# A parallel attention and MLP block: score maxima and v turned on VectorE, key blocks regrouped for it, and a two-class transfer list

## The chip, the cores and the metric

The kernel runs on one core of a Trainium2 chip. Its time is the device time of one execution in microseconds (us), given as the median over several executions. TensorE (PE) does the matrix products, VectorE (DVE) and ScalarE (ACT) the element-wise work, GpSimd (POOL) some additions, and SyncE (SP) only issues transfers. ACT issues transfers too, from the same queue as its other instructions.

## The reference

```python
x = A_x                                   # 1 x 2048 x 448, float32
xn = _layernorm(x, axis=-1)
return x + _A_ref(xn, A_wq, A_wk, A_wv, A_wo) + _B_ref(xn, B_w1, B_w2)

# _A_ref: 16 heads of 28, one k and one v for all of them
q = (x @ wq) as 16 heads;  k = x @ wk;  v = x @ wv
scores = einsum("bhqd,bkd->bhqk", q, k) * 28 ** -0.5
p = softmax(scores);  o = einsum("bhqk,bkd->bhqd", p, v)
return o.reshape(B, S, 448) @ wo

# _B_ref: dense layer with 1792 hidden columns
return relu(x @ w1) @ w2
```

Everything is float32 outside; inside, the products use values split in a high and a low part.

## The kernel before

The 2048 rows are cut in four query blocks of 512 (`NQB`), the 16 heads in four groups of four (`NHG`). A unit `u` is one query block with one head group; there are 16 units, and each works through 16 key blocks of 128 (`NKB`). TensorE's array is used as four groups of 32 rows, one head (or one slice of a product) in each, and the four groups run at the same time.

There are three stages. In the first (0 to 62 us) the rows are normalised and transposed, and q, k and v are projected; the results go out to DRAM (`qscr`) and come back in the layout that the heads need. k stands in `kHL`, high and low part, one column per key; `kD` holds differences of two blocks of 512 keys. In the MLP stage (62 to about 387 us) the 168 tiles of the two dense layers are worked off, and between their matmuls stand 426 of the 1024 matmuls that serve the scores' row maxima, and eight early score tiles. The attention stage (about 388 to 996 us) makes the scores, their exponentials and the products with v, with the other 598 maxima matmuls between; then the end follows.

The row maximum of the scores is needed before the exponential. `max_mm` (L563) multiplies one unit's high-part queries (`qhi`) by 512 keys into a PSUM bank, and a VectorE reduction (L567) takes the maximum over the keys. With the pair form, ACT writes `more` = relu of a product with `kD` (L758) and VectorE combines it with the first bank (L571). When a unit's 64 pieces are done, `max_final` (L574) makes the negated maxima and their rounding remainder, 128 partitions by 32 values, and orders the next `qhi`. `max_rows` (L583) turns these on PE (L588) into 32 rows by 128, ACT copies them out of the bank (L590), and four transfers (L596) put them into two spare rows of each head's part of the query tile `q`; there the third matmul of a score tile, 30 rows high, adds them to the scores. `v_rows` (L537) turns v from rows by head dimension to key order: four PE transposes (L541) and an ACT copy (L543) into `vtile`.

The order of the work is written out by hand. The table `ROWS` (L32) is read one character at a time in the MLP stage: `a` to `h` start tiles on the four row groups, `0` to `3` go on with one matmul, `i` to `l` and `m` to `t` are maxima matmuls, `vA`, `vB`, ... take a job from the list of owed VectorE work, `A` to `D` start early scores, and one `X65` does the maxima rows of unit 0 and v. The table `ORDER` (L116) gives the attention stage: `B4.12.0.3541602` is a burst of 4 score tiles, with maxima matmuls ahead and behind on the named row groups, and the banks; `V` is the product with v for one key block (L827), `R` one `max_rows`, and `r`, `n`, `O`, `f` normalise and project the output.

Transfers (L448) go out on SP's queue, but in the MLP stage they are put on the list `later`, and every tile that ends (`go_on`, L766) issues the first of that list from ACT's queue. The weights' parts `stg`, the unit queries `qhi`, the query tiles `q` and the eight pieces of v share that list. When a tile of the first layer ends, ACT writes the hidden values' high part (`hH` L716) and VectorE the low part (`hL` L718); of the second layer ACT copies the tile (`y` L725) and POOL adds it (L726). Then its bank is free.

Of the kernel before, what the change touches and what calls it, by code (L numbers as in the profile page):

```python
# [17 lines left out]
NU = NQB * NHG  # L18
P_BUFS = 24
# [11 lines left out]

ROWS = """  # L32
    a3b4c5012012012012012d60123012301230123013o73e5s130g4f330213021p2021t0vA021021021p1021t7021vAl0021e6
    10j2vBh40k7f530g313vA021302130vA21302130213vA02130213m021l2q121e4g6vA02h302302vAj730230j12302vA3j202
    3023vA0230k03vAf6h51313vBm713q113vA13i21313vAi013131vBc4a320b120vBd212031203120vA31c03123e4f3vA2l701
    201h1201vA3201320132e2vAj53023j60h42vA03g3j703203f02vAe131203210l521vA0l6g210210h32vA1a7321320132vA0
    13g103120l52f402l61021h0vA02130c313201vA32f20321i5321i1321g7vA31a61230f3230vA120l5120l41021vAl1e0210
    2f60l22vA10h32130k513vA01c4301230f723vA012l1012h6012vA3c2e31320312vA031203120h41vA2031k5i131g63e223j
    0vA0230b32h70213vA02130k513e4vA130c11302103vA201320132i6132m01h22q53f4vA23123e31231vA03k61010h1vAb5c
    703120312vA0312031203120f23k0103k41e53k6vA1031g30h71203vA02f13023123vA1i0321i4h521a23vA210321032013v  # L40
    Ak60130k01h3e71k4vA30f20g531023vA102310231e12vA31203f7k60310k0130g2vA1d4201320132vA0b5320132301c6vA0
    l012h212e4312vB0312031203vA1023102l7m312q0d12vAf431g5a23120312031032vA10h62n7032r0e1320j3320f232013v
    B2013g40132i01vA23e5123f1021l30vA21h20c7130213vA021302f63201320l01g10l4120l312vAe712021h502vA130g210
    321032vA1i032j4a123f7023vA10c33102310vA23102d01e623j2023f102310vB23102130213vA01k430j230f33vA0g11h72
    01321e0vA321032310231k50vAp410t210h1vAc601301320b7321302vA13201h32m513q21g03f623m4123q1123e71230vA12
    031023j2023vAb102h61i5312vAe331k4301g73102vA3f002l2102h110vA2310231k503vA1c430123012h7vA0123e6123023
    10g13b20231vA02h40123a5123vA012301o33013s70d01c6301230123012302vAf43201l7g21012e1l31vA20h61023f5023v
    A10230123e412301l7201l3201l10g0vA102h21e623102vA3102023j70k4vA3b30g531e0231vA02310231021vA30f620p112
    t7vAe212h310231023103k4f003vA1c70312h501230vA123102j6320g3j1302b43vAe7213021302vA1302130c0102vAp6e31
    2t10120h712vA03120312032i23b1vA32a51h402103vA1k6031013k30f73vAe0k21301g13120vA312031203f52vA0p61201t  # L50
    30g41d202130123023n7e12vA3r30230f02h5012301320132e2vA31k60310h110k3vA301k7301g53e412vA3012302f2l60vA
    21l3201h010c1vA3101302b7302vA13201230123m5g213q6213e121302vA1d3021302103vAo6103s43vA3g7f1m5312q2312a
    031vA2031201d42032vA0f330231m2231q6231i5h1g013213e72vB132013201320vAl61g402l5102h0vA0b22301230123vA0
    1g3313021p1e42j5t602f00h721032vA103210321e2vA32103j62030f4k5301c1vA0132e3123102d0vA1203b62031g2032vA
    103210321032102310k5310o731e1s4h2vA10310g03032j5vA032032e62l3vB02f1021l4vA021d501230123vA10o2303s7f0
    03vAc31h102310231e52310vA23012301g6l4012l7012h3a2vA12301302f5302vA130213021l1e021l4021h20vAf33013k70
    13g5vA0132013210h6vA2j10320f23210k43vA1e3c73102310vB231023b102310vA23i51g2d412e7321vB0231023102310vA
    k0310k3313vA1o5a2f73s6013vAg101d0201301230123vAe4j3230j6320f2h72vA1032130213vA02130g01302b5l3021h120
    132vA10321i63g21i732f4i32vA31e023102310vA2310g53012l60vA12i7h2213e121vA32013k30130f0vA3k601h5g4013vA
    120312031320vAb73201d220132i3132e513021vB30b620310g731vA0231231i02vA31212i31d1c5vAe2132031203vA21032  # L60
    n4302r0h70g6j3302f130213vB02130213021h5vAi0132j33e7230f22vA3012301g1l401vA20l021e5h6210vA32102310k33
    01vAc730123e11203vAn4203r02032f503g210d312e73120312vA031203b02031vA20p112e6t41201h72013g301320132vA0
    31203120p521vA0t4k1f7010g0d2vB1e321023102vA31023n4023r10vA2323m5f323q7123a61c1vA301201h0201320vAf223
    0123m713q41g63i5123e121032vB1032103210p3vA01k5t4e01h603f1vAk7031g2031230vB123012p410vA2t50f62l7012h1
    01320vB132a3132013vAc503b720120vA120d42e2132013g3012301230123012301230o6130s0f5310h3g710312e43123012
    vA30n1230r02h50vA2j63023f302310vB23103c210l021vA021h7e52j63023vAf402310k1301c3vA30213e221032vA103210
    2310k0l610c5l11e72h3vA1203f22031203vA12301g43012l0vA012h50j6230f3vA32013210321vAa13210h22103j0203f5v
    Ac60310231e332vA1021h1021302vA30j7230b023e513vA021l20210l4g110vA2l3012e6d712301vA23012301c23vA01230f
    12l5012l4120h0vA12031g703120vA3f22i3123a5123012vA301k4301k130f630vAk31e7h21031vA0g0310231023vA0132i4
    1h52i1312e231vA2031203f7203vA120h610k331i4g513e0213vA20j13203j220vA32b3031c7031vA2031201d4201vA320f5  # L70
    320132vA1e33120310231023vAj10o203s63e7c0vA0h30j5320f432vA301232013201vAd1k601301k2301g3vA320132e0132
    vA0l5120h71203f1vAk60130g413i212vA31231m523f0vAq323123e112031201l6021p2vA0f72t301h01vA3e4k5130g11302
    1vB30213201d320vA132031k6031c530b023vA0120d221321e3vA2310301k1301vAo6031s7031e53vA1c4031203f320l1120
    vA120h012e231k7vA031k603f4031k1vA301301g3vA13021302f5302vA12l7012h401g03i61vA23i1132f232m3vA132h512q
    731vA23e41230123013201vAp60c710t121e02120d32b5032103g2103123012vA3012h70j4230j1320f332vA01321e53210d
    6vA2103c4103f702vA310231e3231023102103vA2j1032032e7j0h5vA023j20g33f6023vB10231023e412d1vA012301g5302
    31vA230123012l7012d001g130j2vA230b3231023vA1e623120l71k50h41g003j2vA203f1203120vA3120312103g3vA1203j
    7203f02i5312e1l2vA1201g60120vAl7120f4h32031vA2i5312e03120vA31203120l212vA0d110c73e3132vA0132031203b5
    2vA01201l22e1120vA12010l0210vAd6c30132e7132vA03120321302f1l4o201h5s01031g60vA12301230f323012vA30123m
    41g13q012312e63f72020l2120h31g503vA10231i03213vA2i4132i112vA1d22e3132013vA02f6302130k013vA0k41h7e513  # L80
    01g2vA30j12302b330vA2132013201vA3k0103k6103c4f20vA120d112e3312vA0312031023vA0n0230r623e22vA30j7203g3
    0320vBf420d5123e121vA302130o6130s7130o2h310s03103g510321320vA1320b7d0021vA32e41301k6310g131023vAf502
    l3102l2102h71vA023103123f002vA310231e52l610k31h40k2130vAg7f103210321e0vA32013201230vA1k6301c330123e7
    vA210l5210d220132vB0b63g001321e32vA31023021302vA130k5130k413i71c1vA21h3a02130vA23f2023102310vAg63012
    l51e12l4102h0vA013201320132vA0132m7312q5f3h12i413g213213e6vB12301320f0l52vA01l4201210vA210l3210d72f1
    3vA01k53013g001vA32e2132012h6j40vA230f72310k33vA10c531021302vA1320b132013201g73i412d0e521302vC130213
    02130vA1o3301s4e73103vAk2f503103g110vB210d6123e0123vA032j4032j2032j70vAh5203203f62vA301c33102310vA2h
    110213a42j2302j730g0j530vA203f320132e6vA132013201302vA1h402n2302r73vAe12j5303g6032f00vBh3210321032vA
    3102310g43210l7210l52102d21vAe32301c630132vA0f432013201d7vA21i5321e23210vA32j1032032vA03b30c013i4213
    vA2e6132012l501vA2l10f2g7012h31vA02310231032vA103f02031201l42i5121e32h6vA10g23j10203f72vA03120321e03  # L90
    vA2103k4013g3013201vA23012a5l1120l2120h0vA1c4032f603201vA32e7132013201h5o1013s3013c2031230123012h401
    vA230j0320f532a3132vB103210210l1vA10f40h21k0vA031g503120132vA1032b60321vA2i731c1e4312031vA203120h3n0
    203r5203f2g6i72312e131vB203120312031vAk50310o431e6s7vA10l001h1g301320vBb532013i7213vAe2213012h61023v
    Aj0032f13021302vA130g51l4201d720132vA0f3320132a013k6031c4l1012vBh50123012301vA2301230132vA01l620f721
    02vBp21e51t10g010h4vA1203j602302b33e72vA1032103210vA3210321032n1a53k60r2h30g7f0302vA310230123e421vA3
    201h50k21301g33012vA30213021320p6120t1j7c20f52h0012vB31e3213021032vA103k1f403c70132e2vA1230123012302
    1d60g510321i1321e732vA102301230f2c33vA01230123i0123vA1i12h7123j5vAe623b430213021vA3021h20k01310vA3k1
    f703103g41vA0321h3021302vA13i52b0321i2g631vAi1123e41230123vA0n7230r5230vA2h00b2321e33210312vA301o130
# [71 lines left out]
def attention_plus_mlp(ctx: ExitStack, tc: tile.TileContext, x, wq, wk, wv, wo, w1, w2, out):  # L170
# [412 lines left out]
    def max_rows(b, between=None):  # L583
# [7 lines left out]
        if between:  # L591
            between()
# [389 lines left out]
```

## Time and profile before

| | |
|---|---|
| median of three runs | 1009.01 us (1007.97 to 1009.62) |
| profiled execution | 1007.41 us |
| its span, first to last instruction | 1005.6 us |
| mean granted TensorE clock | 0.998 |
| PE busy | 995.6 us, 99% |
| DVE busy | 714.6 us, 71% |
| ACT busy | 699.9 us, 70% |
| POOL busy | 248.5 us, 25% |
| DMA, share of 16 engines | 10.3% and 3.1% on the two largest queues |

Busy times are read from one profiled execution. Matmuls overlap and their ends are modelled, so a high share of PE busy time does not say that PE works at its peak. In a row such as `L611 PE MATMUL b<-q,kHL 28*128 28x512 f32` the line of the program comes first, then the engine, the operation, what is written and from what, and the tile. `b` and `o` are PSUM banks. ACTq is the queue of transfers that ACT issues; a row of it says how long the queue was held by the issue.

### The profile page before, as it was taken

What the parts mean: (1) busy time and instruction counts of PE and PEld (TensorE: products, weight loads), DVE (VectorE), ACT (ScalarE), POOL (GpSimd) and SP (SyncE); (2) the same over time, 40 slices, a digit from 0 to 9 for tenths busy, and PEclk for the clock granted to TensorE, in tenths of its full rate; (3) what the DMA queues carried; (4) which work ended last, traced back from release to release, by engine and by line L of the source; (5) the groups of instructions that cost most, each with busy time, mean ns of one, the idle gap of its engine ahead of it and who ended that gap; (6) DMA issues with size and microseconds to landing.
All of it is one profiled execution on the core that took longest, in us unless ns stands there. A gap on an engine that the chain in (4) does not pass through costs nothing.

```text
span 1005.6 us, 28502 instructions
## 1 busy us (share of the span) xinstructions
PE 995.6 (99%) x11704; PEld 634.0 (63%) x11704; DVE 714.6 (71%) x1287; ACT 699.9 (70%) x1359; POOL 248.5 (25%) x251
## 2 busy tenths in 40 slices
PE   9999999999999999999999999999999999999998
PEld 8779999999998996444444445444445443445444
DVE  7649888888887877888888876778775545774202
ACT  5533344434333447888899987899998799997994
POOL 4325464655646335110110110110110110110110
PEclk9999999999999999999999999999999999999999
DMA  7742101101010011101011002010011110000001
GB/s 242 255 138 83 41 13 41 25 30 41 15 41 13 3 34 34 34 24 41 5 44 34 23 33 63 10 44 23 23 34 37 36 34 23 13 13 29 22 13 37
DMA packets 28391, 43.76 MB, mean 44 GB/s; under 512 B 9140, under 2 KB 20084, under 8 KB 28260
## 3 DMA queue, kind: packets, MB, share of 16 engines
q1 hardware_dynamic: 22336, 32.68, 10.3%
q10 hardware_dynamic: 5924, 9.26, 3.1%
q8 instruction: 91, 1.49, 0.6%
q14 instruction: 40, 0.33, 0.1%
HBM read 29.36 MB, written 12.18 MB: 41 GB/s over the span
## 4 chain that ended last, share of the span: by engine, by line
PE 98%; DVE 1%; DMA 1%; ACT 0%; issue 0%; ACTq 0%; POOL 0%; POOLq 0%
PE o L827 25%; PE b L611 25%; PE b L701 23%; PE b L563 9%; PE b L867 4%; PE o L701 4%; PE b L424 3%; PE b L231 1%; PE b L433 1%; PE b L373 1%; PE o L563 1%; PE b L402 0%; DMA qscr<-qs 0%; PE b L588 0%; PE b L911 0%; DMA qhi<-qscr 0%
## 5 line engine op out<-in xcount | busy, mean ns | idle before, releaser
L567 DVE TENSOR_REDUCE nmx<-b 128x1 f32<-128x512 f32 x860 | 551.6, 685 | 154.6 <-PE b L563 130.9
L614 ACT ACTIVATE p<-b 128x512 f32<-128x512 f32 x1016 | 522.6, 611 | 73.1 <-PE b L611 69.5
L611 PE MATMUL b<-q,kHL 28*128 28x512 f32 (+1 forms) x3072 | 335.6, 425 | 0.0
L563 PE MATMUL b<-kHL,qhi 28*128 28x512 f32 x917 | 327.6, 449 | 1.4 <-ACT more L758 1.1
L611 PEld LDWEIGHTS b<-q,kHL 28*128 28x128 f32 (+1 forms) x3072 | 196.5, 183 | 186.6 <-DVE nmx L567 101.2
L701 PE MATMUL b<-xt,w 32*128 32x512 f32 x2058 | 300.2, 393 | 0.0
L701 PE MATMUL b<-w,hH 32*128 32x448 f32 x1552 | 277.9, 369 | 0.0
L827 PE MATMUL o<-p,vtile 128*32 128x512 f32 x2032 | 267.1, 605 | 0.0
L701 PEld LDWEIGHTS b<-xt,w 32*128 32x128 f32 x2058 | 242.9, 183 | 4.1 <-SPq L705 1.0
L701 PE MATMUL b<-w,hL 32*128 32x448 f32 x776 | 211.6, 363 | 0.0
L701 PEld LDWEIGHTS b<-w,hH 32*128 32x128 f32 x1552 | 202.4, 183 | 5.8 <-DVE hL L718 0.9
L563 PEld LDWEIGHTS b<-kHL,qhi 28*128 28x128 f32 x917 | 148.5, 183 | 58.3 <-DVE nmx L567 23.0
L726 POOL TENSOR_TENSOR acc<-y,acc 128x448 f32<-128x448 f32 x112 | 128.0, 1153 | 154.0 <-ACT y L725 153.8
L851 POOL TENSOR_TENSOR on<-rb,oS 128x512 f32<-128x512 f32 x15 | 19.2, 1283 | 518.7 <-DMA rb<-rscr 316.3
L701 PEld LDWEIGHTS b<-w,hL 32*128 32x128 f32 x776 | 122.6, 183 | 0.3
L725 ACT ACTIVATE y<-b 128x448 f32<-128x448 f32 x97 | 52.6, 546 | 92.9 <-PE b L701 76.7
L827 PEld LDWEIGHTS o<-p,vtile 128*32 128x32 f32 x2032 | 42.2, 108 | 77.5 <-issue 71.3
L701 PE MATMUL o<-xt,w 32*128 32x512 f32 x294 | 74.2, 394 | 0.0
L701 PE MATMUL o<-w,hH 32*128 32x448 f32 x240 | 69.9, 370 | 0.0
L758 ACT ACTIVATE more<-b 128x512 f32<-128x512 f32 x55 | 32.8, 599 | 39.1 <-PE b L563 23.2
L701 PEld LDWEIGHTS o<-xt,w 32*128 32x128 f32 x294 | 51.8, 183 | 0.3
L571 DVE CUSTOM_DVE_ANT_0 more<-b,more 128x512 f32<-128x512 f32 x57 | 38.9, 686 | 17.2 <-ACT more L758 16.8
(119 smaller groups left out, 764.0 us busy)
## 6 DMA issues: line engine op xcount, KB each, us to landing
qscr<-qs SPq DMA_DIRECT2D x16, 512.0 KB
q<-qscr SPq DMA_DIRECT2D x12, 512.0 KB
rb<-rscr SPq DMA_DIRECT2D x60, 64.0 KB
out<-acc SPq DMA_DIRECT2D x16, 224.0 KB
acc<-in_A_x SPq DMA_DIRECT2D x14, 224.0 KB
qhi<-qscr SPq DMA_DIRECT2D x11, 256.0 KB
stg<-in_B_w ACTq DMA_DIRECT2D x5, 448.0 KB
q<-qscr ACTq DMA_DIRECT2D x4, 512.0 KB
```

The source lines that it names most:

```text
L424: nc.tensor.matmul(pq, w, xm, start=n == 0, stop=n == len(steps) - 1)
L563: nc.tensor.matmul(pm, qhi[u][rows, s * P : (s + 1) * P], k, start=True, stop=True)
L567: nc.vector.tensor_reduce(dst, pm, axis=AX.X, op=ALU.max)
L571: nc.vector.tensor_tensor_reduce(more, pm, more, 1.0, LEAST, ALU.add, ALU.max, dst)
L611: nc.tensor.matmul(ps, kHL[rows, kt, w, keys], qst[u][rows, s, :], start=k == 0, stop=k == 2)
L614: nc.scalar.activation(p, ps, AF.Exp, scale=SCALE)
L701: mm = nc.tensor.matmul(o, w, m, start=self.left == self.n_mm - 1, stop=self.left == 0)
L725: nc.scalar.activation(y, self.ps[:, 0:D], AF.Copy)
L726: nc.gpsimd.tensor_tensor(a, y, a, op=ALU.add)
L758: nc.scalar.activation(more, d[1], AF.Relu)
L827: nc.tensor.matmul(o_acc[u][RB * j : RB * (j + 1)], vtile[:, kb, :], ps[j], start=kb == 0, stop=kb == NKB - 1)
L867: nc.tensor.matmul(py[:, 0:D], om[:, i * P : (i + 1) * P], wm, start=n == 0, stop=n == len(steps) - 1)
```

## The change

Maxima: `max_final` turns its 128x32 result on VectorE in squares of 32 (L583 of the new program) into `rows`, and four transfers write it to a DRAM tile `nscr`; `max_rows` is now two transfers from `nscr` into `q`. It takes no bank, no PE and no ACT operation. For the first three units it is put on the list at once, after two empty entries (`pause`); the others' stand as `R` in `ORDER`, 13 of them.

v: one VectorE transpose of 128x512 in squares of 32 writes `vtile`, and the fourth query tile is loaded right after it into the freed buffer. For that the key blocks are regrouped: a block of 128 is 32 keys from each of the four blocks of 512, so `kHL` and `kD` have other shapes, and `k_diff` makes the differences in eight POOL operations instead of two.

Transfers: `soon` stands beside `later` and is emptied first; `qhi` and the weights' parts go there. The first three query tiles come ahead of the eight pieces of v on `later`.

Buffers: the exponentials go to three tiles of eight slots instead of 24 single buffers and one for the early ones. Both tables are new throughout: 421 maxima matmuls in the MLP stage and 603 after it; the kinds and counts of all other matmuls are the same but for the 20 transposes.

```diff
-    nc.gpsimd.memset(vtile, 1.0)
-    kHL = cst.tile([P, NQB, 2, QB], F32R, name="kHL")
-    kD = cst.tile([P, NQB // 2, QB], F32R, name="kD")
+    kHL = cst.tile([P, 2, NKB, NQB, RB], F32R, name="kHL")
+    kD = cst.tile([P, 2, TPB, NQB, RB], F32R, name="kD")
...
+    def k_diff(b):
+        hi = kHL[:, 0, :, b].bitcast(F32).rearrange("p (t h k) q -> p t h k q", t=2, h=2)
+        for t in range(2):
+            nc.gpsimd.tensor_tensor(kD[:, t, :, b], hi[:, t, 1], hi[:, t, 0], op=ALU.subtract)
...
-            later.append(lambda: nc.scalar.dma_start(dst, src))
+            (soon if first else later).append(lambda: nc.scalar.dma_start(dst, src))
...
-            transfer(qhi[u].bitcast(F32), queries(u)[:, 0])
+            transfer(qhi[u].bitcast(F32), queries(u)[:, 0], True)
...
-    nc.gpsimd.memset(vt, 0.0)
+    nc.gpsimd.memset(vt, 0.5)
+    for u in range(3):
+        load_q(u)
     for b in range(NQB):
         for g, n in kparts:
...
             transfer(vt[d0 : d0 + n].rearrange("p s q -> p (s q)"), src)
-    load_q(0)
-    load_q(1)
-    load_q(2)
+    pause = [lambda: None] * 2
     later.append(lambda: nc.gpsimd.tensor_tensor(vt[:, 0], vt[:, 0], vt[:, 1], op=ALU.add))
+    later += pause
-    def v_rows(b):
...
+    def v_rows():
+        nc.vector.transpose(vtile.rearrange("p k d -> p (k d)"), vt[:, 0])
+        load_q(3)
+
+    later.append(v_rows)
...
-        nm2[u] = t
+        rows = small.tile([P, RB], F32, name="rows")
+        nc.vector.transpose(rows, t.rearrange("p j s i -> p (j s i)").bitcast(F32))
+        dst = nscr[u].rearrange("j s (i x q) -> x (j s i) q", x=HG, q=RB)
+        for x in range(HG):
+            transfer(dst[x], rows[RB * x : RB * (x + 1)])
+        if while_mlp and u < 3:
+            later.extend(pause)
+            max_rows(u)
         load_qhi(u + 3)
...
+    def max_rows(u):
+        for s in range(2):
+            dst = qst[u].bitcast(F32)[:, 0].rearrange("(j c) q -> j c q", c=RB)
+            transfer(dst[:, DH + s], nscr[u, :, s])
...
+    def score_exp(ps, i):
+        nonlocal n_p
+        if n_p % 8 == 0 and len(p_buf) < 3:
+            p_buf.append((ppool if len(p_buf) == 1 else wpool).tile([P, 8, QB], F32, name="w"))
+        p = p_buf[n_p // 8 % 3][:, n_p % 8]
+        n_p += 1
...
-                        transfer(dst, src)
+                        transfer(dst, src, True)
...
-            if later:
-                later.pop(0)()
+            if soon or later:
+                (soon or later).pop(0)()
```

The order at the first use of unit 6's queries, on PE before. `w`, `xt`, `hH` and `hL` belong to MLP tiles, `b0` to `b7` and `o` are banks, and the number behind a name tells one buffer from another:

```order
L701 MATMUL b6_6429<-w_5539,hL_6360 128x448
L701 MATMUL b3_6472<-w_5539,hH_6359 128x448
L701 MATMUL b0_6370<-xt_353,w_5539 128x512
L701 MATMUL b1_6349<-xt_353,w_5539 128x512
L701 MATMUL b4_6494<-w_5539,hH_6359 128x448 [waits SP_sequencer_49]
L701 MATMUL b3_6472<-w_5539,hL_6360 128x448
L701 MATMUL b4_6494<-w_5539,hH_6359 128x448
L701 MATMUL b0_6370<-xt_353,w_5539 128x512
L701 MATMUL b1_6349<-xt_353,w_5539 128x512
L563 MATMUL o_6607<-kHL_76,qhi_6560 128x512 [waits DMAHW0_49,Activation_49]
```

The first of these rows ends the tile in bank b6. On ACT before, the tile's copy and the transfer that its end issues:

```order
L725 ACTIVATE y_6479<-b5_6333 128x448 [waits PE_49,Pool_49]
L758 ACTIVATE more_6552<-o_6550 128x512 [waits PE_49]
L725 ACTIVATE y_6592<-b6_6429 128x448 [waits PE_49,Pool_49]
L450 DMA qhi_6560<-qscr_65 128x512
L716 ACTIVATE hH_6617<-b1_6349 128x512 [waits PE_49]
```

On ACT now, the transfer of unit 6's queries is `qhi_6347`:

```order
L720 ACTIVATE hH_6362<-b3_6089 128x512 [waits PE_49]
L454 DMA qhi_6347<-qscr_65 128x512
L720 ACTIVATE hH_6362<-b1_6105 128x512 [waits PE_49]
L454 DMA nscr_67<-rows_6345 32x32 [waits DVE_49]
L729 ACTIVATE y_6417<-o_6253 128x448 [waits PE_49,Pool_49]
L454 DMA nscr_67<-rows_6345 32x32 [waits DMAHW5_49]
```

It follows the tile in bank b3 (`b3_6089`), whose last matmul is PE's row 4083; the first use of `qhi_6347` is PE's row 4246. Before, the two stand nine rows apart.

The order in the attention stage, on PE before, behind a burst, with the transpose of one unit's maxima:

```order
L563 MATMUL b5_8908<-kHL_76,qhi_6560 128x512
L563 MATMUL b1_8911<-kHL_76,qhi_6560 128x512
L588 MATMUL b6_8914<-ident_72,nm2_5319 32x128
L827 MATMUL o_8554<-p_8802,vtile_73 32x512
L827 MATMUL o_8554<-p_8783,vtile_73 32x512
```

On DVE now, where a unit's maxima are finished:

```order
L569 TENSOR_REDUCE nmx<-b_8719 128x1
L579 TENSOR_REDUCE nm<-nmx 128x16
L580 CAST nm_8723<-nm 128x4x4
L581 TENSOR_TENSOR nm_8723<-nm,nm_8723 128x4x4
L583 STREAM_TRANSPOSE rows<-nm_8723 128x32
L569 TENSOR_REDUCE nmx<-b_8749 128x1
```

The PE row between the burst and the products with v is gone, and VectorE has one row more per unit.

The order on ACT where v and unit 0's maxima are turned, before:

```order
L758 ACTIVATE more<-b_7849 128x512
L590 ACTIVATE rows<-b_7882 32x128
L543 ACTIVATE vtile<-b_7886 128x4x4x28
L596 DMA q<-rows 2x4x128 x4
L725 ACTIVATE y<-b_7805 128x448
L450 DMA q<-qscr 128x1024
```

On ACT now, at the query load that follows v's transpose, much earlier in the MLP stage:

```order
L729 ACTIVATE y<-b_1461 128x448
L720 ACTIVATE hH<-b_1406 128x512
L454 DMA q<-qscr 128x1024
L720 ACTIVATE hH<-b_1419 128x512
L454 DMA stg<-in_B_w 128x3x256
```

The copies out of the banks and the four transfers in a row are gone; the query load waits there for VectorE's transpose of v.

More of the change, by code (lines that the diff above doesn't have):

```diff
@@ L198, in attention_plus_mlp @@
     rscr = dram.tile([NU, HG, QB], F32, name="rscr")
+    nscr = dram.tile([NU, HG, 2, QB], F32, name="nscr")
     acc = cst.tile([P, NT, D], F32, name="acc")
@@ L442, in queries, with transfer @@
         return qscr[g, b]
-    later = []
+    later, soon = [], []
     while_mlp = False
-    def transfer(dst, src):
+    def transfer(dst, src, first=False):
         if while_mlp:
-            later.append(lambda: nc.scalar.dma_start(dst, src))
+            (soon if first else later).append(lambda: nc.scalar.dma_start(dst, src))
         else:
@@ L575, in max_final @@
         nm = small.tile([P, HG, 1, TPB], F32, name="nm")
-        t = small.tile([P, HG, 2, TPB], F32R, name="nm2", bufs=NU)
+        t = small.tile([P, HG, 2, TPB], F32R, name="nm2")
         nc.vector.tensor_reduce(nm, nmx.pop(u), axis=AX.X, op=ALU.max, negate=True)
@@ L799, in attention_plus_mlp @@
             owe_combine(first_of.pop(r), max_mm(b, r, kD))
-        elif c == "v":
+        else:
             owed.pop(ord(b) - ord("A"))()
-        else:
-            v_bank = next(stream)
-            max_rows(b, lambda: v_rows(v_bank))
-            load_q(3)
-            p_early = wpool.tile([P, 8, QB], F32, name="w")
-    for issue in later:
+    for issue in soon + later:
         issue()
```

309 lines of the change are left out of this document (141 added, 168 removed).

## The prediction

> **What bounds the kernel now.** First the busy times and the chain of waits on the page.
>
> ```profile
> span 1005.6 us, 28502 instructions
> PE 995.6 (99%) x11704; PEld 634.0 (63%) x11704; DVE 714.6 (71%) x1287; ACT 699.9 (70%) x1359; POOL 248.5 (25%) x251
> PE 98%; DVE 1%; DMA 1%; ACT 0%; issue 0%; ACTq 0%; POOL 0%; POOLq 0%
> PE o L827 25%; PE b L611 25%; PE b L701 23%; PE b L563 9%; PE b L867 4%; PE o L701 4%; PE b L424 3%; PE b L231 1%; PE b L433 1%; PE b L373 1%; PE o L563 1%; PE b L402 0%; DMA qscr<-qs 0%; PE b L588 0%; PE b L911 0%; DMA qhi<-qscr 0%
> ```
>
> TensorE (PE) is the path from end to end, so two things can shorten the span: PE work that goes, and the few holes in PE. The windows of the MLP stage show where the holes are (columns: window, its length, then busy us and instructions of PE, PEld, DVE, ACT, POOL, then clock, DMA share, GB/s).
>
> ```profile
> 212.00:262.00 50.00, 50.00 (x879) 48.15 (x875) 44.41 (x82) 17.77 (x32) 27.14 (x25) 1.00 0.10 28
> 262.00:312.00 50.00, 47.56 (x839) 45.99 (x835) 41.32 (x78) 19.89 (x36) 27.43 (x25) 1.00 0.09 27
> 305.00:308.30 3.30, 0.86 (x20) 0.46 (x12) 0.45 (x3) 0.54 (x1) 1.82 (x2) 1.00 0.25 79
> ```
>
> A full window holds 879 matmuls in 50.00 us, 57 ns each. The next holds 40 fewer, and its hole lies at 305: 3.30 us with 0.86 of PE, 2.44 us lost. The chain of waits there, and at a smaller hole later (columns: start, us, what):
>
> ```profile
> 305.45 0.02 ACT y L725
> 305.48 2.63 DMA qhi<-qscr
> 308.11 0.14 issue
> 308.25 0.47 PE o L563
> ...
> 352.18 0.02 issue
> 352.21 1.29 DVE nmx L567 x2
> 353.50 0.65 DVE hL L718
> 354.15 0.01 issue
> 354.16 0.46 PE o L563
> ```
>
> At 305.48 ACT issues unit 6's queries (qhi), and PE needs them nine rows of its order later. At 354.16 the wait is VectorE's (DVE's), for a bank that hL frees.
>
> **Removed: the late queries, −2.5 us.** In the changed order the same transfer is issued 163 PE rows ahead of its first use, 163 × 57 ns = 9.3 us, against 2.63 + 0.14 us of transfer: the hole goes, 2.44 us. The other units' transfers stand as far ahead or further. What cures it is the new table: the owed list was empty when this transfer was issued (ACT issued it as soon as its tile ended), so overtaking by itself would have moved nothing there. The hole at 354 is about 0.4 us (between 0.2, PE's idle time there, and 0.7, the matmuls missing at 57 ns); its order goes too, but DVE at 44.41 of 50 us stays as full, so it may come back elsewhere. I take −0.3.
>
> **Removed: transposes on PE.** Sixteen of the units' maxima (L588), four of v (L541). ACT's timeline around one in the attention stage, at another one, and at the place in the MLP (start, us, engine, line; in brackets idle before):
>
> ```profile
> 494.68 2.07 ACT L614 ACTIVATE p<-b 128x512 f32<-128x512 f32 x4 [0.27 <-PE b L611]
> 496.96 2.06 ACT L614 ACTIVATE p<-b 128x512 f32<-128x512 f32 x4 [0.21 <-PE b L611]
> 498.88 0.26 ACT L590 ACTIVATE rows<-b 32x128 f32<-32x128 f32 x1
> 499.55 2.06 ACT L614 ACTIVATE p<-b 128x512 f32<-128x512 f32 x4 [0.40 <-PE b L611]
> 501.84 2.07 ACT L614 ACTIVATE p<-b 128x512 f32<-128x512 f32 x4 [0.23 <-PE b L611]
> ...
> 361.41 0.27 ACT L590 ACTIVATE rows<-b 32x128 f32<-32x128 f32 x1 [1.05 <-PE b L588]
> 361.84 0.54 ACT L543 ACTIVATE vtile<-b 128x448 f32<-128x448 f32 x1 [0.17 <-PE b L541]
> 361.85 2.84 ACTq L596 DMA_DIRECT2D q<-rows  x4
> 365.43 0.55 ACT L725 ACTIVATE y<-b 128x448 f32<-128x448 f32 x1 [3.04 <-PE b L701]
> 365.45 0.33 ACTq L450 DMA_DIRECT2D q<-qscr  x1
> ```
>
> ```profile
> L588 PE MATMUL b<-ident,nm x16: 283/284/285, 361.1 to 945.1; 128*32 128x128 f32 x16
> 571.22 2.07 ACT L614 ACTIVATE p<-b 128x512 f32<-128x512 f32 x4 [0.18 <-PE b L611]
> 573.79 2.06 ACT L614 ACTIVATE p<-b 128x512 f32<-128x512 f32 x4 [0.39 <-PE b L611]
> 576.04 2.07 ACT L614 ACTIVATE p<-b 128x512 f32<-128x512 f32 x4 [0.18 <-PE b L611]
> 894.71 16.93 ACT L614 ACTIVATE p<-b 128x512 f32<-128x512 f32 x32 [0.16 <-PE b L611]
> 911.50 0.26 ACT L590 ACTIVATE rows<-b 32x128 f32<-32x128 f32 x1
> ```
>
> Groups of four exponentials start 2.28 us apart (494.68 to 496.96) and 2.29 (499.55 to 501.84), but 2.59 with a transpose between: 0.30 us, about L588's own 0.284 us; at the other place 2.57 (571.22 to 573.79) against 2.25. Fifteen of these stand in the attention stage. Some (911.50) fall where exponentials run back to back, 16.93 us for 32, so that ACT paces and only part of the 0.28 counts: I take 0.24 each, −3.6, between 0.1 (−1.5) and 0.30 (−4.5). In the MLP one of L588 and the four of v stand together. They cost between 0.28 us, L588 alone with v's hidden, and 1.2 us, ACT's idle times before L590 and L543 (1.05 + 0.17); I take −0.6. The ACT queue is then shut 2.84 us for four small transfers, and that ends too.
>
> **Added on VectorE: +0.6.** Sixteen 128x32 transposes and one of 128x512, which no trace here shows. Nearest rows:
>
> ```profile
> L567 DVE TENSOR_REDUCE nmx<-b 128x1 f32<-128x512 f32 x860 | 551.6, 685 | 154.6 <-PE b L563 130.9
> L579 DVE TENSOR_TENSOR nm<-nm,nm 128x16 fp32r<-128x16 f32 x16 | 4.5, 283 | 0.6
> L559 DVE MEMSET nmx<- 128x64 f32 x16 | 1.8, 112 | 0.0
> ```
>
> A small operation takes 0.11 to 0.28 us, one over 512 elements 0.69. DVE is 71% busy and its results are late for PE only in places, so of 16 × 0.11–0.28 = 1.8–4.5 us I count 0.3 us (from 0, all of it in DVE's idle time, to 4.5). The large one is followed at once by the issue of the fourth query transfer on ACT, which waits until DVE has turned v, since both use one buffer: what is queued behind it on ACT is the next Relu, for which PE waits with a bank. 0.69 us and whatever DVE has in hand, with ACT idle more than half the time: +0.3 (0 to 1.5). By the Trainium skill ("VectorE: DVE Perf Modes", The three transpose paths) DVE turns a 128x128 bf16 tile in 311 ns and TensorE in 390, in squares of 32 only; by that estimate a 128x32 piece would be under 0.31 us and the sum unchanged; no run shows it yet.
>
> **Moved to ACT's queue: +0.6.** In the MLP stage the maxima of five units now leave by 20 transfers to DRAM, and three units' come back by six: 26 where there were 4, one for each tile that ends. The four cost 2.84 / 4 = 0.71 us each on the queue; 22 × 0.71 = 16 us. Almost all of it lies in ACT's idle time (17.77 to 19.89 of 50 us busy), but a Relu queued behind one comes up to 0.7 us late, and PE and DVE's hL wait for it. Bounds: 0, as tiles end 1.9 us apart and banks leave slack, and 16 us. The row nearest to it is the place at 361.85: ACT shut for 2.84 us cost PE less than 1 us, 0.25 a transfer at most with all four in a row; apart they have slack each time. I take 0.03 each.
>
> **Moved between stages: +0.5.** The tables hold 421 early maxima matmuls for 426, 603 late ones for 598. Early they cost 57 ns each, −0.3. Late, L563's mean is
>
> ```profile
> L563 PE MATMUL b<-kHL,qhi 28*128 28x512 f32 x917 | 327.6, 449 | 1.4 <-ACT more L758 1.1
> ```
>
> 0.449 us, four at a time, 0.11 at the least; with its place in a burst of four row groups not always filled I take 0.16: +0.8.
>
> **At nothing.** The queries now leave ahead of v. Two stretches of the chain early in the MLP stage, and the ACT queue's row that the second names:
>
> ```profile
> 63.33 3.74 DMA qscr<-qs
> ...
> 75.94 0.66 ACTq L450
> ...
> 77.27 0.70 DVE hL L718
> ```
>
> ```profile
> 75.35 1.25 ACTq L450 DMA_DIRECT2D q<-qscr  x1
> ```
>
> A v piece shuts the queue 1.25 us, a query tile 0.33 (365.45): up to 1.25 − 0.33 = −0.9, since the Relu and hL behind it were late for PE. But the first pair of maxima now stands ten matmuls nearer to the 3.74 us wait at 63.33, which stays: 10 × 57 ns = +0.6. I take 0. The key differences, eight smaller POOL operations for two, lie in POOL's idle time (22.86 of 50 us), with the first maxima that read them as cover. SP's small transfers (70 for 60) have the time of two units as theirs. Without that lead one would cost what qhi did, 2.6 us a unit.
>
> **Sum.** −2.5 −0.3 −3.6 −0.6 +0.6 +0.6 +0.5 = −5.3 us. The profiled execution took 1007.41 us (span 1005.6, 1.8 outside it) and would take 1002.1. It is 1.6 us below the median of 1009.01; against that median the sum gives 1003.7, which I predict.
>
> **The rivals.**
> *The new table has holes of its own.* A different order of 9,600 matmuls, with DVE at 41–44 of 50 us; for it, the old table has holes at 305 and at 354. Against it, the two full windows quoted have no hole in PE beside the one at 305, and each transfer of the new order stands well ahead of its use. Three new holes of 1.7 us would bring it to 1008.8: no change. 0.17.
> *Slower: ACT's queue in the MLP stage.* Every small transfer delays a bank. At 0.71 us each in full it is 16 − 0.6 us more than in the sum, 1019; the gain is used up at 0.03 + 5.3 / 22 = 0.27 us a transfer, about what the four in a row cost. Against it: ACT is idle over 60% there. Chance of 0.27 or more 0.12, then about 1013. The Trainium skill ("DMA: Bandwidth & Descriptors", Rules for kernel authors) would have many small transfers coalesced and calls those under 64 KB mostly overhead; 32x32 pieces are 4 KB, so by it this is the side to watch; the 2.84 us for four agrees.
> *The DVE transposes take the place of PE's.* If each of the 11 late ones delays the next maxima by its 0.28 us, 3.1 us come back: 1006.5, at the border. 0.09.
> *It does not do what it says.* If the query transfer is late for another reason (its buffer, not its place), the hole at 305 stays: 1006.2. The trace has ACT's y end and the issue together, so 0.05.
>
> **How the numbers follow.** The forecast has 0.57: from 999.5 (transposes 4.5, queue, DVE and tables at their lower ends) to 1006.5. Differences within 0.2%, 2.0 us, can't be told from none here, so faster means below 1007.0. Faster: 0.57, 0.10 of the 0.14 that the two cases near 1006 have, and 0.04 of the first rival: 0.71. Same: 0.13 of that rival, 0.04 of those two and 0.01 of the slower one: 0.18. Slower: 0.11. For 8 in 10 the range runs from 999.3 to 1009.5.
>
> **What would show it.** No PE wait for qhi; PE at 50 of 50 us in the window around 305; exponentials 2.3 us apart where a unit's maxima return, as elsewhere; STREAM_TRANSPOSE under 0.3 us; ACT's queue with gaps after each small transfer, PE's chain without an ACT row behind one. Wrong would be PE idle on Relu or y behind an nscr transfer, a hole where v is turned, or bursts that wait for DVE behind a transpose.

## The result and the profile after

The changed kernel took 1001.52 us (median of four, 1000.93 to 1001.63), the kernel before 1008.86 us (four, 1007.97 to 1009.62): a ratio of 0.9926, interval 0.9909 to 0.9944. Run again beside three of the experiments, it took 0.994 of the time before (0.9925 to 0.9955). The forecast was 1003.7 us, faster. The profiled execution took 1001.45 us against 1007.41, 6.0 less where the sum had 5.3.

The page of the changed kernel, its first lines and the chain by engine (lines answer to those shown of before; L825 is now the product with v, L607 the scores, L705 the MLP, L565 the maxima):

```profile
span 999.2 us, 28738 instructions
PE 990.1 (99%) x11684; PEld 631.4 (63%) x11684; DVE 720.4 (72%) x1304; ACT 696.3 (70%) x1339; POOL 249.9 (25%) x256
PE 97%; DVE 2%; DMA 1%; ACT 0%; issue 0%; ACTq 0%
```

PE is still the path; VectorE has 2% of the chain where it had 1%. The same window as before around 305 us, then the groups of the new operations (minimum, median, maximum in ns; ACT queue rows first, then the two sizes of VectorE transpose):

```profile
262.00:312.00 50.00, 50.00 (x883) 48.07 (x879) 42.57 (x82) 20.61 (x37) 29.60 (x27) 1.00 0.09 28
```

```profile
L454 ACTq DMA_DIRECT2D nscr<-rows x20: 308/314/467, 146.3 to 353.9; - x20
L454 ACTq DMA_DIRECT2D q<-nscr x6: 483/514/564, 163.0 to 261.2; - x6
...
L583 DVE STREAM_TRANSPOSE rows<-nm x16: 211/211/213, 142.3 to 937.9; 128x32 f32<-128x32 f32 x16
...
L544 DVE STREAM_TRANSPOSE vtile<-q x1: 702/702/702, 100.7 to 100.7; 128x512 f32<-128x512 f32 x1
```

The hole is gone: 883 matmuls where there were 839. A small transfer holds ACT's queue 0.31 us outward and 0.51 back, not the 0.71 taken from four in a row. The transposes have the sizes that were bounded, 0.21 and 0.70 us.

Where the span's 6.4 us went, by the starts of the MLP's last matmul with `hL` and of the last product with v:

| | before | changed | difference |
|---|---|---|---|
| start to the last `hL` matmul | 386.9 | 383.2 | −3.7 |
| from there to the last product with v | 608.5 | 605.8 | −2.7 |

The second line holds something that isn't work. In windows of the kernel before (the last three columns are clock, DMA share, GB/s), and of the changed one:

```profile
390.00:400.00 10.00, 10.00 (x77) 4.97 (x73) 8.27 (x16) 7.25 (x15) 3.35 (x4) 0.83 0.39 84
392.00:395.00 3.00, 3.00 (x25) 1.76 (x23) 2.98 (x5) 2.98 (x7) 1.35 (x1) 1.00 0.19 31
395.00:399.00 4.00, 4.00 (x30) 1.41 (x29) 2.29 (x5) 2.25 (x5) 0.00 (x0) 0.59 0.83 184
399.00:402.00 3.00, 3.00 (x35) 1.20 (x31) 2.32 (x5) 2.25 (x5) 1.98 (x2) 0.98 0.01 2
```

```profile
390.00:400.00 10.00, 10.00 (x107) 4.01 (x99) 9.44 (x19) 7.26 (x15) 3.53 (x2) 1.00 0.38 83
```

Before, the granted clock falls to 0.50 for 3.4 us at 395 us, which is 0.83 over the ten: a loss of 1.7 us. In the changed kernel's profile it does not, neither there nor in the MLP stage. So of the 2.7 us only 1.0 is work, and of the whole 6.4 about 4.7. The executions say the same by their mean clock. Where the changed kernel was run again, those of before with a clock of 0.998 took 1008.0 to 1008.5 us (seven), those of the changed kernel with 0.998 took 1003.2 to 1003.9 (four), and its one with 1.000 took 1001.4. At equal clock the change is worth about 4.8 us. The experiments below are compared "at 0.998" or "at 1.000" in the same way.

### The profile page after: what moved, and what is told of

The parts are those of the page before. It is cut to its first block, busy times and chain, and to the rows that moved or that the text cites. A ratio compares the mean times of both kernels' runs of the same rounds, so it can differ in the third digit from the quotient of the medians.

```text
span 999.2 us, 28738 instructions
## 1 busy us (share of the span) xinstructions
PE 990.1 (99%) x11684; PEld 631.4 (63%) x11684; DVE 720.4 (72%) x1304; ACT 696.3 (70%) x1339; POOL 249.9 (25%) x256
## 4 chain that ended last, share of the span: by engine, by line
PE 97%; DVE 2%; DMA 1%; ACT 0%; issue 0%; ACTq 0%
PE o L825 25%; PE b L607 25%; PE b L705 24%; PE b L565 10%; PE b L865 4%; PE b L428 3%; PE o L705 3%; PE b L437 1%; PE b L370 1%; DVE nmx L569 1%; PE o L565 1%; PE b L399 0%; DMA qscr<-qs 0%; DMA acc<-in_A_x 0%; PE b L909 0%; ACT w L618 0%
## 5 line engine op out<-in xcount | busy, mean ns | idle before, releaser
L618 ACT ACTIVATE w<-b 128x512 f32<-128x512 f32 x1021 | 525.8, 609 | 72.3 <-PE b L607 68.7
L607 PE MATMUL b<-q,kHL 30*128 30x512 f32 (+1 forms) x3063 | 334.3, 425 | 0.3 <-ACT w L618 0.3
L565 PE MATMUL b<-kHL,qhi 28*128 28x512 f32 x900 | 321.4, 452 | 3.1 <-ACT more L762 2.0
L607 PEld LDWEIGHTS b<-q,kHL 30*128 30x128 f32 (+1 forms) x3063 | 196.7, 183 | 182.0 <-DVE nmx L569 100.7
L705 PE MATMUL b<-xt,w 32*128 32x512 f32 x2226 | 306.3, 393 | 0.0
L705 PE MATMUL b<-w,hH 32*128 32x448 f32 x1552 | 275.6, 368 | 0.0
L825 PE MATMUL o<-w,vtile 128*32 128x512 f32 x2048 | 268.2, 603 | 0.0
L705 PEld LDWEIGHTS b<-xt,w 32*128 32x128 f32 x2226 | 255.4, 183 | 3.6 <-issue 0.7
L705 PE MATMUL b<-w,hL 32*128 32x448 f32 x776 | 213.4, 363 | 0.0
L705 PEld LDWEIGHTS b<-w,hH 32*128 32x128 f32 x1552 | 203.2, 183 | 3.9 <-issue 0.6
L565 PEld LDWEIGHTS b<-kHL,qhi 28*128 28x128 f32 x900 | 143.4, 182 | 67.6 <-DVE nmx L569 31.8
L705 PEld LDWEIGHTS b<-w,hL 32*128 32x128 f32 x776 | 123.8, 183 | 0.2
L825 PEld LDWEIGHTS o<-w,vtile 128*32 128x32 f32 x2048 | 42.6, 108 | 80.6 <-issue 76.2
L705 PE MATMUL o<-w,hH 32*128 32x448 f32 x240 | 70.2, 370 | 0.1
L720 ACT ACTIVATE hH<-b 128x512 fp32r<-128x512 f32 x53 | 30.8, 598 | 30.2 <-PE b L705 27.3
L705 PE MATMUL o<-w,hL 32*128 32x448 f32 x120 | 43.5, 363 | 0.0
L705 PEld LDWEIGHTS o<-w,hH 32*128 32x128 f32 x240 | 42.7, 183 | 0.8 <-DVE nmx L569 0.4
```

The costliest lines, as they stand in the source:

```text
L565: nc.tensor.matmul(pm, qhi[u][rows, s * P : (s + 1) * P], k.rearrange("p k b q -> p (k b q)"), start=True, stop=True)
L607: nc.tensor.matmul(ps, keys, qst[u][rows, s, :], start=k == 0, stop=k == 2)
L618: nc.scalar.activation(p, ps, AF.Exp, scale=SCALE)
L705: mm = nc.tensor.matmul(o, w, m, start=self.left == self.n_mm - 1, stop=self.left == 0)
L720: nc.scalar.activation(hH, self.ps, AF.Relu)
L825: nc.tensor.matmul(o_acc[u][RB * j : RB * (j + 1)], vtile[:, kb, :], ps[j], start=kb == 0, stop=kb == NKB - 1)
```

## The experiments

Each was run beside the kernel before. Those that double or leave out small transfers, that repeat VectorE's transposes and that move the pair form's buffers ran on one chip, the others on another.

**The queries one unit earlier, tables unchanged.**

```diff
-    hipool = ctx.enter_context(tc.tile_pool(name="hipool", bufs=3, side="right"))
+    hipool = ctx.enter_context(tc.tile_pool(name="hipool", bufs=4, side="right"))
...
-        load_qhi(u + 3)
+        load_qhi(u + 4)
...
-            for u in range(3):
+            for u in range(4):
                 load_qhi(u)
```

> The kernel before with a fourth buffer for the units' queries, so that each unit's transfer is issued one unit earlier (unit 6's first use then stands 907 matmuls behind its issue, not 6); tables unchanged. Theory (the hole at 305 us is only the late issue): no PE wait for qhi, 2.4 us less, 2.7 with the later ones, about 1006.3 against 1008.9. Rival (something else is late there too, VectorE or a bank, and takes the wait's place): the hole only shrinks, under 1 us gained, 1008 or more.

Measured: 1005.47 us, 0.9956 (0.994 to 0.9973); at a clock of 0.998 1004.0 against 1007.3 to 1009.2. No PE wait for `qhi` is left, and its window is full where that of before, second, is not:

```profile
300.00:310.00 10.00, 10.00 (x186) 9.89 (x182) 8.98 (x21) 4.21 (x8) 4.42 (x5) 1.00 0.09 28
```

```profile
300.00:310.00 10.00, 7.56 (x137) 7.07 (x133) 6.34 (x16) 2.58 (x5) 3.52 (x4) 1.00 0.09 28
```

By the starts of the MLP's matmuls, this one gains 2.8 us on the kernel before at 305 and another 0.5 at 354, 3.3 in all. The second hole, which the prediction had laid to VectorE, was the queries' too: unit 7's stood 44 matmuls ahead of their use, 2.5 us, less than a transfer takes. And the matmul that before started at 354.16, just behind the end of `hL`, here starts at 352.42 while `hL` still runs (0.69 us from 352.09), so it does not wait for `hL`. A fourth buffer alone brings most of what the whole change brings.

**The transposes on PE left out.**

```diff
-        pn = bank(b)
-        nc.tensor.transpose(pn[0:n, 0:P], t, ident)
-        rows = small.tile([n, P], F32, name="rows")
-        nc.scalar.activation(rows, pn[0:n, 0:P], AF.Copy)
+        if between:
+            pn = bank(b)
+            nc.tensor.transpose(pn[0:n, 0:P], t, ident)
+            rows = small.tile([n, P], F32, name="rows", bufs=1)
+            nc.scalar.activation(rows, pn[0:n, 0:P], AF.Copy)
+            row0.append(rows)
+        rows = row0[0]
```

> The kernel before, in which the PE transpose and the ACT copy of the 15 units that return in the attention stage are left out (the first unit's rows are sent to all of them, so their maxima are not the right ones); the transfers stay. Theory: each costs 0.24 us on PE's path, 15 x 0.24 = 3.6 us less, about 1005.3. Rival (they are covered by the exponentials where ACT paces): 1.5 us less, about 1007.4.

Measured: 1008.70 us, 0.9985 (0.9974 to 0.9995); at 0.998 1007.0 against 1007.3 to 1009.2. Nearer to the rival: over the attention stage from 420 us on, the products with v gain only 0.9 us on the kernel before. ACT's timeline at the first place that the prediction quoted:

```profile
495.89 2.07 ACT L617 ACTIVATE p<-b 128x512 f32<-128x512 f32 x4 [0.26 <-PE b L614]
498.17 2.06 ACT L617 ACTIVATE p<-b 128x512 f32<-128x512 f32 x4 [0.21 <-PE b L614]
500.63 2.06 ACT L617 ACTIVATE p<-b 128x512 f32<-128x512 f32 x4 [0.40 <-PE b L614]
502.92 2.07 ACT L617 ACTIVATE p<-b 128x512 f32<-128x512 f32 x4 [0.23 <-PE b L614]
```

With the transpose the third group started 2.59 us after the second, without it still 2.46, not 2.28. The product with v behind it comes 0.27 us earlier, but half of that is waited off in the next group. The 0.30 read from the gap was not what its removal is worth. At a few other places steps of 0.22 to 0.32 us come back, which the last section takes up.

**The new code with the old tables.**

```diff
 ROWS = """
-    a3b4c5012012012012012d60123012301230123013o7i2j03s1e53f3g403vA120312012vA0p1120t2120vA12l00120120l7v
+a3b4c5012012012012012d60123012301230123013o73e5s130g4f330213021p2021t0vA021021021p1021t7021vAl0021e6
...
 ORDER = """
-    B3..0.4025 R V1 B7.111.000.6341052360451 V1 B3.011.1.2035641 V1 B4.3.12.2305461 V1 B3.0.00.523601 V2
+V2 B4.000..5361204 B6.111.00.53260134502 B3.1.11.163542 V1 B4.11.0.0614325 V1 B3.0.00.603154 
...
```

The word `X65` is left out, `R` has no number, and the two `R` of units 1 and 2, which return by themselves, are gone.

> The changed kernel with both tables of the kernel before (without the bank words for the transposes, and without the two returns that now come by themselves). Theory: the transposes' 3.6 us and the 0.6 us of the place in the MLP stage are gained, less 0.6 us for VectorE's and 0.6 for ACT's queue; the hole at 305 us stays, 2.4 us, since unit 6's queries stand 6 matmuls ahead of their use again: about 1006, with the hole in the trace. Rival 1 (the whole gain comes from the new tables): 1008.9. Rival 2 (the whole gain comes from the mechanism, overtaking cures the hole): 1001.5 and no wait for qhi.

Measured: 1008.58 us, 0.999 (0.998 to 1.000); at 0.998 1007.3 to 1007.9 against 1007.3 to 1009.2. PE's waits:

```profile
PE o L565 <- DMA qhi<-qscr: 2.4, 1, 2.4
PE b L565 <- DMA qhi<-qscr: 2.3, 1, 2.3
```

The hole at 305 stays, as the theory had it. Overtaking is in this kernel and does not cure it; the order does. The second wait is new. It lies at 411 us, in the attention stage, where the kernel before has no wait for `qhi`. SP's queue there:

```profile
408.18 3.30 SPq L456 DMA_DIRECT2D nscr<-rows  x4
411.59 0.36 SPq L456 DMA_DIRECT2D qhi<-qscr  x1
```

The four transfers of a unit's turned maxima hold the queue for 3.30 us, and the next unit's queries leave behind them; before, with nothing ahead of them, they left at 405.50.

The time is nearer to rival 1 than to the theory: at 0.998 it is about 1 us under the kernel before, not 3. But that is what is left after the 2.3 us which the new code loses under the old order. Without them it would be about 3, the theory's size. Of this, 1.1 us lie at the wait at 66 to 69 us, ahead of every transpose, and that wait varies by 0.8 us among profiles of kernels that are alike up to there. What the mechanism is worth by itself is therefore not shown.

**One list, nothing overtakes.**

```diff
-            (soon if first else later).append(lambda: nc.scalar.dma_start(dst, src))
+            later.append(lambda: nc.scalar.dma_start(dst, src))
```

> The changed kernel with one list: nothing overtakes. Unit 6's queries then stand 29 matmuls (1.7 us) ahead of their use, unit 7's 87 (5 us), against 2.8 us for the transfer. Theory: a hole of about 1.1 us at unit 6 and no other, about 1002.6 against 1001.5. Rival (overtaking is worth nothing): 1001.5. Rival (weights behind the small transfers come late too): over 1004.

Measured: 1004.97 us, 0.9945 (0.9929 to 0.9962); at 1.000 1002.9 and 1003.1 against 1000.9 to 1001.6 of the changed kernel. Its chain:

```profile
303.78 2.71 DMA qhi<-qscr
306.49 0.14 issue
306.63 0.47 PE b L565
```

The hole is back at unit 6 and nowhere else (against the changed kernel's, ACT's starts fall back 1.6 us there). In the changed kernel's own order overtaking is thus worth about 1.5 us. That it is needed only since the change itself puts 26 small transfers on the list is argued: no run has one list without them.

**The small transfers doubled, and left out.**

```diff
-            transfer(dst[x], rows[RB * x : RB * (x + 1)])
+            twice(dst[x], rows[RB * x : RB * (x + 1)])
...
-            transfer(dst[:, DH + s], nscr[u, :, s])
+            twice(dst[:, DH + s], nscr[u, :, s])
...
+    def twice(dst, src):
+        if while_mlp:
+            n = dst.shape[-1] // 2
+            f = lambda: [nc.scalar.dma_start(dst[..., h], src[..., h]) for h in (slice(0, n), slice(n, 2 * n))]
+            later.append(f)
+        else:
+            nc.sync.dma_start(dst, src)
```

> The changed kernel with each of the 26 small transfers of the MLP stage split into two halves, issued one behind the other at the same place: 26 more on ACT's queue. The changed kernel's profile has 0.31 us of queue for one to nscr and 0.51 for one from it. Theory (ACT's queue has slack): 0.03 us each, under 1 us in all, 1002.3 at most. Rival (a small transfer costs the path what it holds the queue): 26 x 0.36 = 9 us, about 1010.

Measured: 1004.63 us, 0.9957 (0.9944 to 0.997); at 0.998 1003.5 to 1005.3. From 80 us to the end of the MLP stage ACT's starts fall 0.7 us behind the changed kernel's, 0.03 us for each added transfer.

```diff
-        for x in range(HG):
-            transfer(dst[x], rows[RB * x : RB * (x + 1)])
-        if while_mlp and u < 3:
-            later.extend(pause)
-            max_rows(u)
+        if u >= 3:
+            for x in range(HG):
+                transfer(dst[x], rows[RB * x : RB * (x + 1)])
```

> The changed kernel without the 18 small transfers of units 0 to 2 in the MLP stage (their scores are then made without the maxima). Theory: 18 x 0.03, 0.5 us less, about 1001.0. Rival (they are what the MLP stage still pays): 18 x 0.36 = 6.5 us less, about 995.

Measured: 1004.96 us, 0.9957 (0.9944 to 0.997). In the MLP stage, where the 18 are left out, ACT's starts keep their distance to the changed kernel's from 72 us to the end: they cost nothing. The kernel is slower for another reason: a half-clock stretch at 68 us (1.7), and 2.4 us that it loses in the attention stage, in nine steps (last section). Both runs say that ACT's queue had slack; the slower rival is out.

**Each small VectorE transpose three times, and 15 of the 16 left out.**

```diff
-        nc.vector.transpose(rows, t.rearrange("p j s i -> p (j s i)").bitcast(F32))
+        for _ in range(3):
+            nc.vector.transpose(rows, t.rearrange("p j s i -> p (j s i)").bitcast(F32))
```

> The changed kernel with every 128x32 transpose on VectorE done three times: 32 more of 0.211 us, 10 in the MLP stage and 22 after it. Theory (VectorE is late for PE only in places): a tenth of it, 0.7 us, about 1002.2. Rival (each delays the next maxima and PE waits): 6.8 us, about 1008.3.

Measured: 1008.67 us, 1.0005 (0.9988 to 1.0023); at 1.000 1006.3 and 1006.5, 4.9 us above the changed kernel's 1001.5. In the MLP stage it falls back 2.2 us in five steps, one at each unit, for ten more transposes: 0.22 each, all of their time. After it 3.1 us for 22, 0.14 each. Why, the chain of the changed kernel shows at unit 1:

```profile
171.50 1.20 DVE hL L722 x2
172.69 1.21 DVE nmx L569 x2
173.90 0.02 issue
173.92 0.23 DVE nm L579
174.15 0.02 issue
174.18 0.50 DVE nm L580
174.67 0.02 issue
174.70 1.08 DVE nm L581
175.78 0.02 issue
175.80 0.21 DVE rows L583
176.01 0.58 DVE nmx L569
176.60 0.04 issue
176.64 0.47 PE b L565
```

VectorE is the chain for 5 us there: the end of a unit is a run of small operations ahead of the reductions that free the banks, and the transpose is one more in it.

```diff
-        rows = small.tile([P, RB], F32, name="rows")
-        nc.vector.transpose(rows, t.rearrange("p j s i -> p (j s i)").bitcast(F32))
+        if u == 0:
+            rows = small.tile([P, RB], F32, name="rows", bufs=1)
+            nc.vector.transpose(rows, t.rearrange("p j s i -> p (j s i)").bitcast(F32))
+            row0.append(rows)
+        rows = row0[0]
```

> The changed kernel without 15 of its 16 small VectorE transposes (the first unit's rows are sent for all units, so the maxima are not the right ones). Theory formed on the run with three of each, which took 4.9 us more for 32 at the same clock, 0.15 each: 2.3 us less than the changed kernel. The prediction's size (0.3 us for all 16): no difference.

Measured: 1000.48 us, 0.9911 (0.9894 to 0.9927), beside 0.994 of the unaltered one. Its profile stands 2.1 us ahead of the changed kernel's at the end. Of this 0.5 us are there by 72 us, ahead of the first transpose at 142, so they are the wait at 66 to 69 us and not the transposes; 1.1 us come between there and the first products with v, 0.5 later. The executions with a clock of 1.000 differ by 1.0 (1000.2 and 1000.8 to 1001.5). The transposes cost 1.0 to 1.6 us of the gain, not 0.3.

**The buffers of the pair form apart.**

```diff
     hpool = mlp.enter_context(tc.tile_pool(name="hpool", bufs=2))
+    mpool = mlp.enter_context(tc.tile_pool(name="mpool", bufs=2))
...
-        more = dpool.tile([P, QB], F32, name="more")
+        more = mpool.tile([P, QB], F32, name="more")
```

> The changed kernel with the two buffers of ACT's relu of the pair form in memory of their own, which the first stage does not use, so that the first pair needs not wait for the last transfer to qscr (the wait of 3.99 us from 63.14, PE idle 2.0 us behind it). Theory: the 2.0 us go, about 999.5. Rival (the query loads or hL are late next and take most of it): under 0.7 us gained, 1000.8 or more.

Measured: 999.68 us, 0.9902 (0.9887 to 0.9916), the fastest complete kernel. The window after the first stage's end, of the changed kernel and of this one:

```profile
62.00:70.00 8.00, 6.00 (x89) 4.84 (x87) 3.82 (x8) 1.59 (x3) 2.47 (x3) 1.00 0.23 88
```

```profile
62.00:70.00 8.00, 8.00 (x129) 7.25 (x128) 5.74 (x12) 1.64 (x3) 2.82 (x3) 1.00 0.22 85
```

The 2.0 us are gained (at 1.000 999.4 and 1000.0 against 1001.5), and nothing takes their place in the MLP stage.

**The changed kernel again.**

> The changed kernel unaltered, beside the next three on one chip, to compare them with it. The half-clock stretch of 3.9 us that the kernel before shows at 395 us is absent in the changed kernel's profile. Theory (that belongs to the order at the start of the attention stage): absent again at 390 to 400, and 0.993 of the time before. Rival (it was chance): it is there, and the ratio is 0.995.

Measured: 1003.37 us, 0.994 (0.9925 to 0.9955). The stretch at 395 is absent again, as the first theory has it, but one stands at 70 us, behind the 2 us in which PE waits. The profiles agree to 0.3 us in the whole attention stage.

**v ahead of the queries, and the fourth query load later.**

```diff
-    for u in range(3):
-        load_q(u)
     for b in range(NQB):
         for g, n in kparts:
...
+    for u in range(3):
+        load_q(u)
     pause = [lambda: None] * 2
```

> The changed kernel with the eight pieces of v ahead of the three query tiles on the list, as before the change. Prediction: a v piece holds ACT's queue 1.25 us where a query tile holds it 0.33, just where Relus free banks: 0.9 us more at most. Rival: no difference, under 0.4 us.

Measured: 1003.04 us, 0.9936 (0.9922 to 0.9951), no difference from the unaltered 0.994. The v piece does make the Relu behind it late, by 0.7 us at 78.08, but most of that is made up within 2 us.

```diff
         nc.vector.transpose(vtile.rearrange("p k d -> p (k d)"), vt[:, 0])
+        later.extend(pause)
         load_q(3)
```

> The changed kernel with the fourth query load two tile ends later than v's transpose, so that ACT's queue doesn't wait for VectorE (ACT idle 1.10 us at 102.64). Prediction: 0.3 us less. Rival (banks have slack there): no difference; 1.1 us less at the most.

Measured: 1003.85 us, 0.9952 (0.9929 to 0.9975). Nothing is gained in the MLP stage; ACT's idle time there, 1.09 us before the Relu at 104.41, is the wait for a reduction, not for the load. In the attention stage this kernel loses 1.9 us in seven steps, though nothing of that stage was edited.

## Why the prediction was right, and where its terms were wrong

**Right.** The time is inside the range and near the forecast, the hole at 305 went, it went because of the order and not of overtaking, and the slower rival (ACT's queue) did not come true. Two rivals came true in part: the new table has a hole of its own, 0.7 us at 176, and VectorE's transposes take back some of what PE's gave.

**The sum's terms.**

- *The late queries, −2.5 and −0.3 for the hole at 354:* 2.8 and 0.5 measured. The step that failed is the reading of the second hole: the chain named VectorE's `hL`, which ended last before PE went on, but PE was waiting for the queries.
- *The transposes on PE, −3.6:* mis-sized most. Left out alone, the fifteen are worth 0.9 to 1.3 us, less than the 1.5 that the prediction set as the least. The gap they open between groups was read rightly, 0.30 us, but the step from the gap to the saving failed: half of it is waited off in the next group, and for what was not isolated.
- *The place with five transposes in the MLP, −0.6:* 0.2. With the new code and the old tables, PE's matmuls stand 0.96 us behind the kernel before ahead of that place, at 361 us, and 0.75 behind it.
- *Small VectorE operations, +0.3 for all 16:* 1.0 to 1.6 us. The average share of VectorE was used where the end of a unit should have been read: there VectorE ends the wait.
- *ACT's queue, +0.6:* next to nothing as it stands (18 left out change nothing), 0.03 each when doubled, which is the prediction's figure.
- *Queries ahead of v, 0, and the load behind v's transpose, +0.3:* no difference in both. In the first the −0.9 of the queue thus did not come; the +0.6 that was set against it, for the first maxima standing nearer to the wait at 66 to 69 us, may have: between 62 and 70 us PE is idle for 2.00 us in the changed kernel's profile and 1.40 in that of the kernel before. But this idle time runs from 1.25 to 1.88 in the profiles of the old code and order and from 1.36 to 2.18 in those of the new ones that keep the buffers of `more`, so it is not shown.
- *More maxima late, +0.5:* not measured by itself.

These sizes give −3.3 for the queries, −1.1 and −0.2 for the transposes and +1.3 for VectorE, −3.3 in all against about −4.8 at equal clock. The rest, some 1.5 us, includes the maxima moved between the stages (predicted +0.5) and what the new order of bursts, the regrouped keys and the exponentials' new buffers bring; the runs did not take these apart. That the sum came so near has a part of luck: the transposes and VectorE were taken some 3.9 us too well, the queries, ACT's queue, the load and this rest about 3.4 us too badly.

**Not in the sum.** The stretch at half clock near 395 us. Each of the four profiles with the old tables has one that begins between 393 and 398 us, and no profile of the changed order has one there, bar the kernel with `more` apart, at 400. The ratio measured first, 0.9926, is 7.3 us, 2.5 more than the 4.8 us of work; this stretch is 1.7 of the 2.5 in the profiles compared. That the order decides whether it comes is likely by this count, and not shown.

## What to carry to other kernels

Look for a late transfer by its distance: matmuls between issue and first use, times the time of one, against the transfer's own, and count what stands ahead of it on its queue; a hole that seems another engine's can be a transfer's as well. The gap that an operation opens was an upper bound of what its removal saved: at the place shown, 0.30 us of gap gave 0.13. Leave the operation out once and measure. And price small operations on a second engine at the place where that engine is waited for, not by its mean share.

## What the runs showed of the hardware

**Half clock without a long pause.** In these profiles the granted clock falls to 0.50 for 3.41 us, which costs 1.7 us, and twice for 10.24 us, which costs 5.1 (at 393 us in the kernel with the queries one unit earlier, at 400 in the one with `more` apart). One of 3.41 us follows the wait of PE at 66 to 69 us in nine of the ten experiments' profiles in which PE is idle there for over 1 us, but neither in the first profile of the changed kernel nor in that of the kernel before, which have that wait too. In the rerun of the changed kernel:

```profile
66.00:69.00 3.00, 0.82 (x14) 0.65 (x15) 0.97 (x3) 0.60 (x1) 1.17 (x2) 1.00 0.02 8
69.00:70.00 1.00, 1.00 (x21) 0.88 (x14) 0.68 (x2) 0.60 (x1) 0.92 (x2) 1.00 0.00 0
70.00:73.00 3.00, 3.00 (x32) 2.94 (x32) 2.41 (x6) 0.00 (x0) 1.11 (x1) 0.50 0.00 0
```

The one at 395 in the kernel before follows no pause in PE's busy time, only 25 matmuls in the 3 us before it, where 35 stand behind it. The Trainium skill ("TensorE: Matmul & The Clock Gate", Part 1) tells of a half rate after an idle window of some 3.4 us, the windows running freely. The traces agree on the windows: a stretch lasts 3.41 us or three times that, and the full clock between two stretches lasts a whole number of them (389.12 us, 114 of them, in the kernel before; 61.44 us, 18, in four of the others). That it comes in some executions and not in others would suit them. That 2 us of waiting or less, or thin work without a pause, is enough is not in it; what decides here stays open.

**Steps of some 0.3 us from the place of an instruction.** Two kernels with the same order in the attention stage, the one with the fourth load later and the changed kernel run again, first and second (ACT's timeline):

```profile
517.87 2.06 ACT L619 ACTIVATE w<-b 128x512 f32<-128x512 f32 x4 [0.46 <-PE b L566]
520.12 2.07 ACT L619 ACTIVATE w<-b 128x512 f32<-128x512 f32 x4 [0.18 <-PE b L608]
```

```profile
518.18 2.07 ACT L618 ACTIVATE w<-b 128x512 f32<-128x512 f32 x4 [0.21 <-PE b L607]
520.50 2.06 ACT L618 ACTIVATE w<-b 128x512 f32<-128x512 f32 x4 [0.26 <-PE b L607]
```

In the first of them the group at 517.87 starts 0.27 us late, with PE's matmuls before it unchanged. Counted among ACT's records in the trace, all seven late ones of that kernel stand at the same place of every 256, and seven of the nine in the kernel without the 18 transfers at another. So something in ACT's stream recurs each 256 records, and shows only where it meets the first exponential of a group; against the changed kernel, ACT's stream has one record less in the one and 21 less in the other, all ahead of that stage, which shifts what meets such a place.

That ACT's instructions are fetched in such pieces would explain it. On a queue of instructions (q14 on the page) a packet of 8 KB starts 0.65 to 0.98 us behind each of the first seven, and 0.65 to 1.09 us behind each of the other seven. But such packets start about every 128 records, so only every other one has a late exponential ahead of it, and no run moved them by themselves: it is argued, not shown. It moved kernels here by up to 2.4 us, as much as most of the edits.
